# Attention with a state, then a two-layer MLP: weights cast by POOL from an fp32 staging ring, all loads on one queue

## The chip, the cores and the metric

The kernel runs on one core of one Trainium2 chip. The time is device microseconds of one execution; the figure for the kernel before is the median of three runs. A core has TensorE (PE in the profile), VectorE (DVE), ScalarE (ACT), GpSimd (POOL) and SyncE (SP). DMAs are issued by SP, by ACT and by POOL, and are carried by 16 DMA engines that they share.

## The reference

For each of 8 batches and 8 heads there are 512 tokens `x` and 32 state rows `state`, 64 wide. The tokens read the states, the states read the tokens, and all results (544 rows of 512 per batch, 4352 in all) go through a two-layer MLP with a leaky ReLU. Everything that comes in is fp32.

```python
scores = scale * x @ state^T            # per batch and head, 512 x 32
a      = softmax(scores);   xread = a @ state
scores2 = scale * state @ x^T           # 32 x 512
a2     = softmax(scores2);  sread = a2 @ x
rows   = concat([xread, sread])         # 4352 x 512
h      = rows @ moe_w_in                # 512 x 2048
out    = maximum(0.01 * h, h) @ moe_w_out   # 2048 x 512
```

## The kernel before, in words

The weights stay in SBUF as bf16 for the whole run: `w_in_bf` (128 partitions, 4 row blocks, 2048 columns) and `w_out_bf` (16 row blocks of 128 rows, 512 columns). The first product is folded: for each batch `a_m` multiplies the states by a 512-column chunk of w_in (line 389), which gives `M`, and `ff1` then multiplies `M` by the probabilities `aT` (line 410), so that xread itself is never formed. `piece` (line 438) does a quarter of the second product, four row blocks of w_out for one tile of 128 tokens. The 256 rows of sread go through `ff1_s` (line 421) at the end.

The instructions of every engine are in the order written in the code (a manual schedule); semaphores are put in by the framework. Batch 0 is done in a start-up of its own: four loads `xf` of 256 KB on SP, cast by VectorE (line 139), transposed on TensorE, scores, row maxima that are split into two bf16 parts `hi` and `lo` (lines 535 and 538), exponentials, probabilities. Between these come `a_m` for batches 0 and 1 as the four column chunks of w_in arrive, `ff1_0`, and then, for batch 1, two casts of `x1` by VectorE (line 687), transposes on TensorE (line 705, tile `pxt`), and the scores (line 253). From there on the loop over batches 2 to 7 runs 16 steps each: `ff1`, one piece of an earlier or of this batch, and at set steps the attention of the next batch. x of batch 2 is cast by ScalarE, that of later batches by POOL (`cast_all`, line 132), and its transpose is a DMA on SP. The states of batches 2 and 3 come by eight small loads on SP (`load_state(0)`, line 201), are scaled by VectorE (line 207) and transposed by a DMA (`st_t`, line 212).

At the start POOL issues the loads, in this order: four of w_in, each 512 rows by 512 columns; w_out row blocks 0 to 1; x of batch 1 in two halves (`x1`); w_out 2 to 3 and 4 to 7; first half of x of batch 2; w_out 8 to 11; second half of x of batch 2; w_out 12 to 13 and 14 to 15. The weight loads change fp32 to bf16 in the transfer, straight into `w_in_bf` and `w_out_bf`. x of batches 3, 4 and 5 is loaded on SP in one piece of 1 MB, that of 6 and 7 on POOL. Stores of the output are SP's.

Of the kernel before, what the change touches and what calls it, by code (L numbers as in the profile page):

```python
# [27 lines left out]
def kernel(  # L28
# [24 lines left out]
    VEC, SCA, POO = nc.vector.tensor_copy, nc.scalar.copy, nc.gpsimd.tensor_copy  # L53
# [5 lines left out]
    nc.scalar.dma_start(  # L59
        st0f[:], state[0:2].rearrange("b h n d -> (b h n) d").rearrange("(p r) d -> p r d", r=4)  # L60
    )
    xf = [consts.tile([P, 2, 2 * P], FP32, name="xf", tag=f"xf{q}") for q in range(NK)]
    xv = x[0].rearrange("h (p t) d -> p h (t d)", t=NT)
    for q in range(NK):
        nc.sync.dma_start(xf[q][:], xv[:, 2 * q:2 * q + 2])

    idle = consts.tile([P, S], BF16, name="idle")
    nc.vector.memset(idle[:], 0.0)
# [24 lines left out]
    w_in_bf = wpool.tile([P, NK, DFF], BF16, name="w_in_bf")  # L93
    w_out_bf = wpool.tile([P, 16, DM], BF16, name="w_out_bf")
    xs, xt, xl = {}, {}, {}

    def load_x(b, eng):
        xl[b] = xpool.tile([P, H, NT * D], FP32, name="xl", tag="xl", bufs=2)
        eng.dma_start(xl[b][:], x[b].rearrange("h (p t) d -> p h (t d)", t=NT))

    def load_x_half(b, u):
        if u == 0:
            xl[b] = xpool.tile([P, H, NT * D], FP32, name="xl", tag="xl", bufs=2)
        nc.gpsimd.dma_start(
            xl[b][:, NK * u:NK * (u + 1)],
            x[b, NK * u:NK * (u + 1)].rearrange("h (p t) d -> p h (t d)", t=NT),
        )

    def open_xb(b):
        if b == 2:
# [8 lines left out]
        h = 2 * (k % 2)  # L121
        return a.xb[k // 2][:, t, h:h + 2, :].rearrange("p h d -> p (h d)")

    def cast_x(b, h0, h1, copy):
        u = h0 // NK
        copy(
            xs[b][u][:, :, h0 - NK * u:h1 - NK * u].rearrange("p t h d -> p h t d"),
            xl[b][:, h0:h1].rearrange("p h (t d) -> p h t d", t=NT),
        )

    def cast_all(b):
        nc.gpsimd.tensor_copy(  # L132
            xt[b][:].rearrange("p t h d -> p h t d"),
            xl[b][:].rearrange("p h (t d) -> p h t d", t=NT),
        )

    def cast_x0(q, copy):
        v = q % 2
        copy(
            xs[0][q // 2][:, :, 2 * v:2 * v + 2].rearrange("p t h d -> p h t d"),  # L140
            xf[q][:].rearrange("p h (t d) -> p h t d", t=NT),
        )

    def load_w_in(c):
        nc.gpsimd.dma_start(  # L145
            w_in_bf[:, :, DM * c:DM * (c + 1)],
            moe_w_in[:, DM * c:DM * (c + 1)].rearrange("(k p) f -> p k f", p=P),
        )

    def load_w_out_rows(j0, j1):  # L150
        nc.gpsimd.dma_start(  # L151
            w_out_bf[:, j0:j1, :], moe_w_out[P * j0:P * j1, :].rearrange("(j p) f -> p j f", p=P)
        )

    def load_w_out(c):
        load_w_out_rows(4 * c, 4 * (c + 1))

    def spin(n, tag, w=S):
        p = psum.tile([P, S], FP32, name="pspin", tag=tag, bufs=2 if tag in ("ph", "py") else 1)
# [59 lines left out]
    def a_open(a, b):  # L219
        a.b = b  # L220
        a.xb = xs[b]
        if b == 2:
            t = att.tile([P, 2, NT, 2, P], BF16, name="xT", tag="xT")
            a.xTh = [t[:, u] for u in range(2)]
        else:
            t = att.tile([P, NT, NK, P], BF16, name="xT", tag="xT")
            a.xTh = [t[:, :, 2 * u:2 * u + 2] for u in range(2)]
        a.xT = t
# [7 lines left out]
    def a_xt_half(a, u):  # L236
        nc.sync.dma_start_transpose(
            a.xTh[u].rearrange("p t k q -> p (t k) q"),
            a.xb[u].rearrange("p t h d -> p (t h d)"),
        )  # L240
# [28 lines left out]
    def block_sub(flat, m1, n):  # L269
        m1b = att.tile([P, n, NS], FP32, name="mrowb", tag="mrowb", bufs=1)  # L270
        nc.vector.transpose(m1b[:], m1[:, :, None].to_broadcast([P, n, NS]))  # L271
        sh = att.tile([P, n * NS], FP32, name="sh", tag="sh")
        nc.vector.tensor_tensor(  # L273
            out=sh[:], in0=flat, in1=m1b[:].rearrange("p c j -> p (c j)"), op=ALU.subtract,
        )
        return sh
# [100 lines left out]
    def a_m(a, c, tag):  # L377
        if c == 0:
            a.M = mpool.tile([P, 2, DFF], BF16, name="M", tag="M")
        if tag in ("ph", "py", "phpy"):  # L380
            pm = [psum.tile([P, DM], FP32, name="pm", tag=t) for t in (tag[:2], tag[-2:])]
            at = [t[:] for t in pm]
        else:
            pm = psum.tile([P, 2, DM], FP32, name="pm", tag=tag, bufs=1)
            at = [pm[:, g, :] for g in range(2)]
        for k in range(NK):
            for g in range(2):
                v, r = (k // 2, 2 * (k % 2) + (g ^ (k // 2))) if a.b == 0 else (g, k)
                nc.tensor.matmul(  # L389
                    at[v][NS * r:NS * (r + 1)],  # L390
                    lhsT=st_of(a, g, k),
                    rhs=w_in_bf[D * g:D * (g + 1), k, DM * c:DM * (c + 1)],
                    start=True, stop=True,
                )
# [80 lines left out]
    a0, a1, a2 = att_of[:3]  # L475
# [91 lines left out]

    for c in range(4):
        load_w_in(c)
    load_w_out_rows(0, 2)  # L570
    x1 = [consts.tile([P, NK, 2 * P], FP32, name="x1", tag=f"x1{u}") for u in range(2)]
    for u in range(2):
        nc.gpsimd.dma_start(  # L573
            x1[u][:], x[1, NK * u:NK * (u + 1)].rearrange("h (p t) d -> p h (t d)", t=NT)
        )
    load_w_out_rows(2, 4)
    load_w_out(1)
    load_x_half(2, 0)
    load_w_out(2)
    load_x_half(2, 1)  # L580
    for v in range(2):
        load_w_out_rows(12 + 2 * v, 14 + 2 * v)
    a0.aT = att.tile([P, 2, S], BF16, name="aT", tag="aT")
    open_xb(1)
    a_open(a1, 1)
    for q in range(2):
        cast_x0(q, VEC)
# [24 lines left out]
    q = [recip0(0)]  # L612
# [62 lines left out]
    for j, tag in ((4, "ph"), (6, "big"), (8, "py"), (10, "big"), (12, "py"), (14, "ph")):  # L675
        t, bk = open_ff1_0(tag)
# [7 lines left out]
            m_halves(a0, 3, "ph")  # L684
            a_max2(a0)
    for u in range(2):
        VEC(  # L687
            a1.xb[u].rearrange("p t h d -> p h t d"),
            x1[u][:].rearrange("p h (t d) -> p h t d", t=NT),
        )  # L690
    nc.vector.memset(stf[0][:, 0, D - 1:D + 1], 0.0)
    load_state(0)

# [6 lines left out]
    for u in range(2):  # L700
        ps = psum.tile([P, NT, 2, P], BF16, name="pxt2", tag="ph")
        for t in range(NT):
            for v in range(2):
                h = NK * u + 2 * v
# [14 lines left out]
        piece(0, h0, i, 1)  # L719
    open_xb(2)  # L720
    a_open(a2, 2)
    cast_x(2, 0, 4, SCA)
    a_xt_half(a2, 0)
    m_evict(a1, 2, a_m(a1, 2, "ph"), SCA)
    a_exp(a1)
    for i in (2, 3):
        piece(0, h0, i, 1)
    m_evict(a1, 3, a_m(a1, 3, "ph"), SCA)
    cast_x(2, 4, 8, SCA)
    for g in range(2):  # L730
        a_exp2(a1, g)
    a_xt_half(a2, 1)
# [49 lines left out]
    for b in range(2, B):  # L782
        hT = hpool.tile([P, 16, S], BF16, name="hT", tag="hT")
# [58 lines left out]

    hs = hpool.tile([P, 16, B * NS], BF16, name="hs", tag="hs", bufs=1)
    b = B - 1
    order = [(0, 3), (1, 3), (2, 0), (2, 1), (2, 2), (2, 3)]
    for s in range(8):
# [41 lines left out]
```

## Time and profile before

| | us |
|---|---|
| three runs, median (lowest to highest) | 216.83 (216.08 to 217.03) |
| profiled execution: span of its instructions | 214.6 |
| median of the runs less that span (start and end around the instructions) | 2.2 |
| TensorE busy in it | 206.1 (96%) |
| ScalarE, VectorE, POOL busy in it | 139.1, 97.7, 25.4 |
| weight and x loads that POOL issues at the start: issue of the first, of the last | 2.83, 21.93 |

The profiled execution's own time is known by its span, 214.6 us; the runs stand 2.2 us above it. In a row of the timeline the first number is the start in us from the span's begin, the second the duration; "x4" says that four instructions are merged, and a bracket tells how long the engine had stood idle and what ended that. In the table by windows the columns are the stretch, its length, busy time of PE, weight loads, DVE, ACT and POOL with their instruction counts, the granted clock, the share of the 16 DMA engines that was busy, and GB/s moved. A row of a DMA on POOL or SP shows the issue; the landing is later. Bytes of a casting transfer are counted as they land, in bf16.

### The profile page before, as it was taken

Reading aid. Unit: us, or ns where it says so; the run is one execution under the profiler, and the core shown is the slowest. Engines: PE = TensorE matmul, PEld = TensorE weight load, DVE = VectorE, ACT = ScalarE, POOL = GpSimd, SP = SyncE. Lnnn points to the kernel's source line nnn. Section 1 sums busy time; section 2 is a strip of 40 time slices with the busy share of each in tenths; the row PEclk is TensorE's granted clock in tenths of the full one; section 3 lists DMA queues with packets and bytes.
Section 4 is the critical chain, followed back from the end, with each engine's and each line's share of the span. In section 5 each row is a group of like instructions: output and inputs, shape, how many; then the busy total and the mean of one; then the engine's idle time right before and its main releaser. Section 6 shows DMA issues by size and latency. Waiting matters only on the chain.

```text
span 214.6 us, 3685 instructions
## 1 busy us (share of the span) xinstructions
PE 206.1 (96%) x1479; PEld 96.5 (45%) x1504; DVE 97.7 (46%) x149; ACT 139.1 (65%) x263; POOL 25.4 (12%) x39
## 2 busy tenths in 40 slices
PE   7789999999999999999999999999999999999993
PEld 2533434344454444444444444444444455466542
DVE  2666687698748235741784095706580000000001
ACT  3578675898788476856696579647774756464420
POOL 8724100030032040521000000000000000000000
PEclk9999999999999999999999999999999999999999
DMA  6999999576992987394216321422124110111113
GB/s 205 207 206 295 257 253 113 126 270 124 241 217 79 200 243 244 89 276 89 87 52 138 59 99 52 100 47 101 48 68 79 74 74 2 49 52 49 49 49 101
DMA packets 38400, 27.70 MB, mean 129 GB/s; under 512 B 24560, under 2 KB 33136, under 8 KB 38384
## 3 DMA queue, kind: packets, MB, share of 16 engines
q1 hardware_dynamic: 32864, 18.95, 35.4%
q0 software_dynamic: 5376, 8.39, 17.4%
q8 instruction: 12, 0.20, 0.4%
q10 hardware_dynamic: 144, 0.13, 0.3%
q14 instruction: 4, 0.03, 0.1%
HBM read 17.30 MB, written 8.91 MB: 122 GB/s over the span
## 4 chain that ended last, share of the span: by engine, by line
PE 86%; DMA 7%; POOL 3%; ACT 1%; issue 1%; DVE 0%; POOLq 0%; ACTq 0%
PE py L438 50%; PE ph L410 22%; DMA x<-in_x_dram 7%; PE ph L421 3%; PE pm L389 3%; PE pyw L438 3%; PE psr L362 2%; PE pyh L462 2%; POOL w_in_bf L145 1%; PE sc L253 1%; ACT M L403 0%; ACT hT L415 0%; POOL x L573 0%; POOL w_out_bf L151 0%; DVE xb L687 0%
## 5 line engine op out<-in xcount | busy, mean ns | idle before, releaser
L438 PE MATMUL py<-w_out_bf,hT 128*128 128x512 bf16 x446 | 116.7, 380 | 1.0
L415 ACT ACTIVATE hT<-ph 128x512 bf16<-128x512 f32 x112 | 66.5, 602 | 41.7 <-PE ph L410 41.0
L438 PEld LDWEIGHTS <-hT 128*128 128x128 bf16 x496 | 46.7, 98 | 57.2 <-issue 5.3
L410 PE MATMUL ph<-aT,M 128*128 128x512 bf16 x221 | 64.9, 379 | 0.2
L410 PEld LDWEIGHTS <-M 128*128 128x128 bf16 x224 | 21.7, 98 | 27.1 <-issue 1.4
L447 ACT COPY ysb<-py 128x512 f32<-128x512 f32 x31 | 18.1, 585 | 10.7 <-PE py L438 10.7
L263 DVE TRANSPOSE_TENSOR_REDUCE mrow<-sc 128x32 f32<-128x1024 f32 x7 | 8.8, 1250 | 33.7 <-PE sc L253 33.7
L467 DVE COPY ysh<-pyh 128x384 f32<-128x384 f32 x1 | 0.6, 557 | 49.0 <-PE pyh L462 49.0
L132 POOL CAST xb<-xl 128x2048 bf16<-128x2048 f32 x5 | 9.4, 1890 | 58.9 <-DMA xl<-in_x_dram 48.2
L285 DVE TRANSPOSE_TENSOR_REDUCE r<-e 128x32 f32<-128x1024 bf16 x7 | 8.7, 1245 | 11.9 <-ACT e L280 11.9
L403 ACT CAST M<-pm 128x1024 bf16<-128x1024 f32 x13 | 13.2, 1013 | 1.2 <-PE pm L389 0.7
L319 ACT ACTIVATE e<-sc,mcol 128x512 bf16<-128x512 f32 x16 | 11.2, 706 | 0.0
L313 DVE TENSOR_REDUCE mcol<-sc 128x2 f32<-128x1024 f32 x8 | 9.7, 1214 | 0.0
L425 ACT ACTIVATE hs<-ph 128x256 bf16<-128x256 f32 x16 | 6.0, 384 | 4.6 <-PE ph L421 4.4
L294 DVE STREAM_TRANSPOSE qb<-qh 128x1024 bf16<-128x1024 bf16 x7 | 8.7, 1245 | 0.2
L271 DVE STREAM_TRANSPOSE mrowb<-mrow 128x1024 f32<-128x1024 f32 x7 | 8.7, 1245 | 0.2
L273 DVE TENSOR_TENSOR sh<-sc,mrowb 128x1024 f32<-128x1024 f32 x7 | 8.6, 1225 | 0.2
L401 DVE CAST M<-pm 128x512 bf16<-128x512 f32 x10 | 6.4, 686 | 4.9 <-PE pm L389 4.9
L403 DVE CAST M<-pm 128x1024 bf16<-128x1024 f32 x7 | 8.5, 1215 | 0.0
L421 PE MATMUL ph<-sr_t,w_in_bf 128*128 128x256 bf16 x64 | 8.3, 273 | 0.0
L438 PE MATMUL pyw<-w_out_bf,hT 128*128 128x512 bf16 x31 | 7.7, 380 | 0.1
L389 PE MATMUL pm<-w_in_bf,st_t 64*32 64x512 bf16 x192 | 7.6, 379 | 0.0
(97 smaller groups left out, 158.0 us busy)
## 6 DMA issues: line engine op xcount, KB each, us to landing
out_dram<-ysb SPq DMA_DIRECT2D x31, 256.0 KB, 2.4
xl<-in_x_dram SPq DMA_DIRECT2D x3, 1024.0 KB, 6.6
w_in_bf<-in_moe_w_in_dram POOLq DMA_DIRECT2D x4, 512.0 KB, 10.4
xl<-in_x_dram POOLq DMA_DIRECT2D x2, 1024.0 KB, 6.7
xf<-in_x_dram SPq DMA_DIRECT2D x4, 256.0 KB, 3.8
w_out_bf<-in_moe_w_out_dram POOLq DMA_DIRECT2D x4, 256.0 KB, 13.9
x<-in_x_dram POOLq DMA_DIRECT2D x2, 512.0 KB, 15.3
w_out_bf<-in_moe_w_out_dram POOLq DMA_DIRECT2D x2, 512.0 KB, 15.4
```

Of the source, the lines that this page charges most:

```text
L132: nc.gpsimd.tensor_copy(xt[b][:].rearrange("p t h d -> p h t d"), xl[b][:].rearrange("p h (t d) -> p h t d", t=NT),)
L263: nc.vector.tensor_reduce(out=m1[:], in_=flat.rearrange("p (c j) -> p c j", j=NS), axis=AX.X, op=ALU.max, apply_transpose=True,)
L271: nc.vector.transpose(m1b[:], m1[:, :, None].to_broadcast([P, n, NS]))
L313: nc.vector.tensor_reduce(out=a.m2[:], in_=a.sc[:], axis=AX.X, op=ALU.max, negate=True)
L319: nc.scalar.activation(out=a.e2[:, g], in_=a.sc[:, g, :], func=AF.Exp, bias=a.m2[:, g:g + 1], accum_out=a.r2[:, g:g + 1],)
L389: nc.tensor.matmul(at[v][NS * r:NS * (r + 1)], lhsT=st_of(a, g, k), rhs=w_in_bf[D * g:D * (g + 1), k, DM * c:DM * (c + 1)], start=True, st ...
L403: copy(a.M[:, :, cols], pm[:])
L410: nc.tensor.matmul(ph[:], lhsT=a.M[:, g, P * j:P * (j + 1)], rhs=a.aT[:, g, :], start=(g == 0), stop=(g == 1),)
L415: nc.scalar.activation(out=hT[:, j, :], in_=ph[:], func=AF.Prelu, scale=1 / SCALE, alpha=0.01)
L421: nc.tensor.matmul(ph[:, :n], lhsT=w_in_bf[:, k, P * j:P * (j + 1)], rhs=sr_t[:, k, :], start=(k == 0), stop=(k == NK - 1),)
L438: nc.tensor.matmul(y.py, lhsT=hT[:, j, P * i:P * (i + 1)], rhs=w_out_bf[:, j, :], start=(j == 0), stop=(j == 15),)
L447: copy(ysb[:], ys[b, i].py)
```

## The change

All start-up loads go to SP and arrive as fp32. A pool `ring` of eleven buffers, each 4 KB a partition (512 KB), takes the place of `xf`, `x1` and `xl`. A weight load is a half of the former w_in chunk (two row blocks by 512 columns) or two row blocks of w_out; POOL then casts it from the ring into `w_in_bf` or `w_out_bf`. The order of the tensors is the old one: w_in in eight halves, w_out 0 to 1, x of batch 1 in two halves, w_out 2 to 7, half of x of batch 2, w_out 8 to 11, the other half, w_out 12 to 15; then SP's list goes on with the states of batches 2 and 3. x of every batch is now loaded and cast in two halves, on the queues and engines as before but for those that left POOL's start-up list. A buffer of the ring is loaded again when its cast is done: `x1`'s first half waits for VectorE's casts of `xf`, the loads from w_out 2 on for POOL's casts of w_in. The tile `sh` has one buffer instead of two, and `hs` shares the two buffers of `hT`.

```diff
+    ring = ctx.enter_context(tc.tile_pool(name="ring", bufs=11))
+    HALF = NK * 2 * P
+    def stage():
+        return ring.tile([P, HALF], FP32, name="ring", tag="ring")
+    def x_half(b, u, eng):
+        t = stage()
+        eng.dma_start(t[:].rearrange("p (h c) -> p h c", h=NK),
+            x[b, NK * u:NK * (u + 1)].rearrange("h (p t) d -> p h (t d)", t=NT))
+        return t
+    xf = [stage() for _ in range(2)]
...
     def load_x(b, eng):
-        xl[b] = xpool.tile([P, H, NT * D], FP32, name="xl", tag="xl", bufs=2)
-        eng.dma_start(xl[b][:], x[b].rearrange("h (p t) d -> p h (t d)", t=NT))
+        for u in range(2):
+            load_x_half(b, u, eng)
...
+    def weights(dst, src):
+        t = stage()
+        v = t[:].rearrange("p (j f) -> p j f", j=2)
+        nc.sync.dma_start(v, src)
+        nc.gpsimd.tensor_copy(dst, v)
     def load_w_in(c):
-        nc.gpsimd.dma_start(
-            w_in_bf[:, :, DM * c:DM * (c + 1)],
-            moe_w_in[:, DM * c:DM * (c + 1)].rearrange("(k p) f -> p k f", p=P),
-        )
+        cols = slice(DM * c, DM * (c + 1))
+        v = moe_w_in[:, cols].rearrange("(k p) f -> p k f", p=P)
+        for k in range(0, NK, 2):
+            weights(w_in_bf[:, k:k + 2, cols], v[:, k:k + 2])
...
-        sh = att.tile([P, n * NS], FP32, name="sh", tag="sh")
+        sh = att.tile([P, n * NS], FP32, name="sh", tag="sh", bufs=1)
...
     for c in range(4):
         load_w_in(c)
-    load_w_out_rows(0, 2)
-    x1 = [...]
-    load_w_out_rows(2, 4)
-    load_w_out(1)
-    load_x_half(2, 0)
-    load_w_out(2)
-    load_x_half(2, 1)
-    for v in range(2):
-        load_w_out_rows(12 + 2 * v, 14 + 2 * v)
+    load_w_out(0, 2)
+    load_x(1, nc.sync)
+    load_w_out(2, 8)
+    load_x_half(2, 0, nc.sync)
+    load_w_out(8, 12)
+    load_x_half(2, 1, nc.sync)
+    load_w_out(12, 16)
...
-    hs = hpool.tile([P, 16, B * NS], BF16, name="hs", tag="hs", bufs=1)
+    hs = hpool.tile([P, 16, B * NS], BF16, name="hs", tag="hT")
```

More of the change, by code (lines that the diff above doesn't have):

```diff
@@ L61 @@
     )
-    xf = [consts.tile([P, 2, 2 * P], FP32, name="xf", tag=f"xf{q}") for q in range(NK)]
+    ring = ctx.enter_context(tc.tile_pool(name="ring", bufs=11))
[4 more added lines that the diff above has]
+        t = stage()
+        eng.dma_start(
+            t[:].rearrange("p (h c) -> p h c", h=NK),
+            x[b, NK * u:NK * (u + 1)].rearrange("h (p t) d -> p h (t d)", t=NT),
+        )
+        return t
+    xf = [stage() for _ in range(2)]
     xv = x[0].rearrange("h (p t) d -> p h (t d)", t=NT)
     for q in range(NK):
-        nc.sync.dma_start(xf[q][:], xv[:, 2 * q:2 * q + 2])
+        v = q % 2
+        nc.sync.dma_start(
+            xf[q // 2][:, S * v:S * (v + 1)].rearrange("p (h c) -> p h c", h=2),
+            xv[:, 2 * q:2 * q + 2],
+        )
     idle = consts.tile([P, S], BF16, name="idle")
@@ L97, in load_x, with load_x_half @@
     def load_x(b, eng):
-        xl[b] = xpool.tile([P, H, NT * D], FP32, name="xl", tag="xl", bufs=2)
-        eng.dma_start(xl[b][:], x[b].rearrange("h (p t) d -> p h (t d)", t=NT))
-    def load_x_half(b, u):
-        if u == 0:
-            xl[b] = xpool.tile([P, H, NT * D], FP32, name="xl", tag="xl", bufs=2)
-        nc.gpsimd.dma_start(
-            xl[b][:, NK * u:NK * (u + 1)],
-            x[b, NK * u:NK * (u + 1)].rearrange("h (p t) d -> p h (t d)", t=NT),
-        )
+        for u in range(2):
+            load_x_half(b, u, eng)
+    def load_x_half(b, u, eng):
+        xl[b, u] = x_half(b, u, eng)
     def open_xb(b):
@@ L122, in pair_of, with cast_x @@
         return a.xb[k // 2][:, t, h:h + 2, :].rearrange("p h d -> p (h d)")
-    def cast_x(b, h0, h1, copy):
-        u = h0 // NK
+    def cast_x(b, u, copy):
         copy(
-            xs[b][u][:, :, h0 - NK * u:h1 - NK * u].rearrange("p t h d -> p h t d"),
-            xl[b][:, h0:h1].rearrange("p h (t d) -> p h t d", t=NT),
+            xs[b][u].rearrange("p t h d -> p h t d"),
+            xl[b, u][:].rearrange("p (h t d) -> p h t d", h=NK, t=NT),
         )
     def cast_all(b):
[L132 to L135, printed above, removed]
+        for u in range(2):
+            cast_x(b, u, nc.gpsimd.tensor_copy)
     def cast_x0(q, copy):
@@ L140, in cast_x0, with load_w_out @@
             xs[0][q // 2][:, :, 2 * v:2 * v + 2].rearrange("p t h d -> p h t d"),
-            xf[q][:].rearrange("p h (t d) -> p h t d", t=NT),
+            xf[q // 2][:, S * v:S * (v + 1)].rearrange("p (h t d) -> p h t d", h=2, t=NT),
         )
-    def load_w_in(c):
-        nc.gpsimd.dma_start(
-            w_in_bf[:, :, DM * c:DM * (c + 1)],
-            moe_w_in[:, DM * c:DM * (c + 1)].rearrange("(k p) f -> p k f", p=P),
[L148 to L156, printed above, removed]
+    def weights(dst, src):
[3 more added lines that the diff above has]
+        nc.gpsimd.tensor_copy(dst, v)
+    def load_w_in(c):
+        cols = slice(DM * c, DM * (c + 1))
+        v = moe_w_in[:, cols].rearrange("(k p) f -> p k f", p=P)
+        for k in range(0, NK, 2):
+            weights(w_in_bf[:, k:k + 2, cols], v[:, k:k + 2])
+    def load_w_out(j0, j1):
+        v = moe_w_out.rearrange("(j p) f -> p j f", p=P)
+        for j in range(j0, j1, 2):
+            weights(w_out_bf[:, j:j + 2, :], v[:, j:j + 2])
     def spin(n, tag, w=S):
@@ L569 @@
         load_w_in(c)
-    load_w_out_rows(0, 2)
[L571 to L575, printed above, removed]
-    load_w_out_rows(2, 4)
-    load_w_out(1)
-    load_x_half(2, 0)
-    load_w_out(2)
-    load_x_half(2, 1)
-    for v in range(2):
-        load_w_out_rows(12 + 2 * v, 14 + 2 * v)
+    load_w_out(0, 2)
[5 more added lines that the diff above has]
+    load_w_out(12, 16)
     a0.aT = att.tile([P, 2, S], BF16, name="aT", tag="aT")
@@ L686 @@
     for u in range(2):
[L687 to L690, printed above, removed]
+        cast_x(1, u, VEC)
     nc.vector.memset(stf[0][:, 0, D - 1:D + 1], 0.0)
@@ L721 @@
     a_open(a2, 2)
-    cast_x(2, 0, 4, SCA)
+    cast_x(2, 0, SCA)
     a_xt_half(a2, 0)
@@ L728 @@
     m_evict(a1, 3, a_m(a1, 3, "ph"), SCA)
-    cast_x(2, 4, 8, SCA)
+    cast_x(2, 1, SCA)
     for g in range(2):
```

## The prediction

> **What bounds the kernel now.** I read the page first, then the chain in order of time for the first 45 us, then the timeline of that stretch, then busy time by window.
>
> ```profile
> span 214.6 us, 3685 instructions
> ...
> PE 206.1 (96%) x1479; PEld 96.5 (45%) x1504; DVE 97.7 (46%) x149; ACT 139.1 (65%) x263; POOL 25.4 (12%) x39
> ...
> PE 86%; DMA 7%; POOL 3%; ACT 1%; issue 1%; DVE 0%; POOLq 0%; ACTq 0%
> ```
>
> TensorE is busy for 206.1 of 214.6 us. The whole program cannot gain more than the 8.5 us between them, and the chain gives DMA only 7%. The next view says where that 7% lies.
>
> ```profile
> 7.40 15.65 DMA x<-in_x_dram
> 23.05 0.02 issue
> 23.07 0.69 DVE xb L687
> ...
> 23.82 0.62 PE pxt L705 x8
> ```
>
> It is one piece: the second half of batch 1's x (line 573) lands at 23.05, stands in its queue behind all of w_in, and VectorE's cast and TensorE's transposes follow it. After that the chain is TensorE almost alone. So only the first 41 us can be touched by how inputs arrive; they are a race between TensorE and the loads. TensorE's side of the race, the starts that need a new input:
>
> ```profile
> 10.72 0.41 PE L389 MATMUL pm<-w_in_bf,stbd 64*32 64x512 bf16 x8
> ...
> 12.76 0.41 PE L389 MATMUL pm<-w_in_bf,stbd 64*32 64x512 bf16 x8 [0.24 <-DMA w_in_bf<-in_moe_w_in_dram]
> ...
> 16.39 0.41 PE L389 MATMUL pm<-w_in_bf,stbd 64*32 64x512 bf16 x8 [0.52 <-DMA w_in_bf<-in_moe_w_in_dram]
> ...
> 18.93 0.41 PE L389 MATMUL pm<-w_in_bf,stbd 64*32 64x512 bf16 x8
> ...
> 22.89 0.61 PE L705 MATMUL pxt<-ident,xb 128*128 128x128 bf16 x8
> ...
> 23.82 0.62 PE L705 MATMUL pxt<-ident,xb 128*128 128x128 bf16 x8 [0.33 <-DVE stf L691]
> ...
> 25.14 0.59 PE L438 MATMUL pyw<-w_out_bf,hT 128*128 128x512 bf16 x2
> ```
> ```profile
> 26.67 2.75 PE L438 MATMUL py<-w_out_bf,hT 128*128 128x512 bf16 x11
> ...
> 31.86 1.90 PE L438 MATMUL py<-w_out_bf,hT 128*128 128x512 bf16 x8
> ...
> 33.60 3.62 PE L438 MATMUL pyw<-w_out_bf,hT 128*128 128x512 bf16 x15
> ...
> 40.60 0.41 PE L253 MATMUL sc<-xT,st_t 64*32 64x512 bf16 x8
> ```
>
> The four w_in column chunks are needed at 10.72, 12.76, 16.39 and 18.93; the second and third came late by 0.24 and 0.52. By the order of the pieces in the code, w_out's rows 2 to 3 are needed at 25.14, rows 4 to 7 near 27.6 (three matmuls into the row at 26.67), rows 8 to 11 at 31.86, rows 14 and 15 near 36.2 (the last four of the row at 33.60). At 40.60 batch 2's scores need its transposed x and states.
>
> **The stream of loads.** What leaves: 14 issues by POOL (four for w_in, six for w_out, four for x), the weights cast on the way. What comes: 20 loads of 512 KB in fp32 on SP (16 of weights, four of x), in the same order of tensors, behind the four xf loads. How fast is SP's queue in fp32?
>
> ```profile
> 3.00:5.00 2.00, 1.92 (x16) 0.67 (x15) 0.76 (x2) 0.23 (x1) 2.00 (x3) 1.00 1.08 373
> 8.00:12.00 4.00, 3.08 (x112) 1.96 (x112) 2.30 (x10) 1.95 (x5) 1.70 (x3) 1.00 1.24 206
> 44.75:46.50 1.75, 1.75 (x9) 0.74 (x8) 1.75 (x3) 1.59 (x3) 1.39 (x1) 1.00 1.06 402
> 74.50:77.00 2.50, 2.50 (x13) 1.15 (x12) 0.00 (x0) 1.04 (x3) 0.00 (x0) 1.00 1.10 351
> ```
>
> The last column is GB/s. From 8 to 12 us the casting transfers land 206 GB/s of bf16, which is 412 of fp32 read: the number to hold. SP's queue moves 373 (xf) and 351 (xl) when x comes in rows of 1 KB, and 402 where the output is stored in rows of 2 KB. The trace has no fp32 load in rows of 2 KB, which is what the weights are. The row it is nearest to by length is the store, so I take 402 for the weights, 1.30 us a half, and 360 for x, 1.46 us. The low end is 351 for all, 1.49 us. There is a lower one, not taken:
>
> ```profile
> xl<-in_x_dram SPq DMA_DIRECT2D x3, 1024.0 KB, 6.6
> xf<-in_x_dram SPq DMA_DIRECT2D x4, 256.0 KB, 3.8
> ```
>
> 768 KB more take 2.8 us more, 281 GB/s; but those loads start on a queue that had stood idle or full of transposes, and the xf stream that the new loads join does not.
>
> ```profile
> 4.28 0.47 DVE L139 CAST xb<-xf 128x512 bf16<-128x512 f32 x1 [0.33 <-DMA xf<-in_x_dram]
> 6.46 0.46 DVE L139 CAST xb<-xf 128x512 bf16<-128x512 f32 x1 [0.24 <-DMA xf<-in_x_dram]
> ...
> L132 POOL CAST xb<-xl 128x2048 bf16<-128x2048 f32 x5 | 9.4, 1890 | 58.9 <-DMA xl<-in_x_dram 48.2
> ```
>
> xf lands one by one from 4.28 to 6.46, so the stream's clock stands at 6.44 when it ends, and each half adds its term. POOL's cast of 2048 elements takes 1.89 us; 1024 take 0.95, and I allow 1.1 with the two hand-overs. It is under 1.30, so POOL keeps up and adds 1.1 once behind each landing, not a sum of sixteen. Ready times: w_in chunks 6.44 + 2 x 1.30 + 1.1 = 10.14, then 12.74, 15.34, 17.94. Batch 1's x (nine weight halves, then two of x, no POOL cast) lands at 21.06, against 23.05. Then w_out rows 2-3 are ready at 23.5, 4-7 at 26.1, 8-11 at 30.1, 14-15 at 34.2. Against the needs, nothing is late, the 0.52 at 16.39 goes, and so does batch 1's x. What is late next is TensorE itself: the first transposes go at 22.89 - 0.52 = 22.37, the second at once behind them when VectorE has cast the second half (22.85), and that is 23.82 - 22.85 = 0.97 us won. That would be all of the gain: from there TensorE has no gap.
>
> **What POOL's casts do to VectorE.** Between 7.8 and 19 us POOL is now casting 0.95 of every 1.30 us, where it issued DMAs. Has VectorE paid for POOL before?
>
> ```profile
> 6.62 1.59 POOL L573 DMA_DIRECT2D x<-in_x_dram  x2
> ...
> 7.74 0.48 DVE L535 CAST hi<-m 128x16 bf16<-128x16 f32 x1
> ...
> 9.59 0.17 DVE L535 CAST hi<-m 128x16 bf16<-128x16 f32 x1
> ...
> 9.80 0.18 DVE L538 TENSOR_TENSOR lo<-m,hi 128x16 bf16<-128x16 f32 x1
> ```
> ```profile
> 65.83 1.59 POOL L207 TENSOR_SCALAR stb<-stf 128x512 bf16<-128x512 f32 x1 [2.96 <-DMA stf<-in_state_dram]
> ...
> 65.98 0.57 DVE L327 TENSOR_SCALAR r<-r 128x2 f32<-128x2 f32 x1
> ```
> ```profile
> L327 DVE TENSOR_SCALAR r<-r x8: 160/163/573, 38.5 to 157.4; 128x2 f32<-128x2 f32 x8
> ```
>
> Twice: `hi` took 0.48 beside a busy POOL and 0.17 beside an idle one, and the one slow `r` of eight (573 against 163 ns) began 0.15 us into a POOL instruction. So a small VectorE operation beside POOL costs 0.3 to 0.4 more, and at most the rest of the POOL cast, 0.95. The two splits (`hi`, `lo`, at 7.74 and 9.59) lie on TensorE's way to the first w_in product at 10.72. The first half lands at 7.74, so POOL's first two casts run about 7.85-8.8 and 9.15-10.1. I take one block of 0.6 that stays: the first `lo` waits to 8.85, the maxima behind it slip, and the second split then falls into the gap after the second cast. Bounds 0 and 1.5 (both casts in full, less the gap).
>
> The Trainium skill (SBUF — State Buffer, "Who interferes with whom") says that a cast or a two-input operation of VectorE and any GpSimd operation take one port pair as an exclusive lock for the whole instruction, the first to start winning. By that the block would be the rest of the cast, 0.6 here; the two slow rows above fit it, though 0.57 is less than the 1.59 of the POOL instruction beside it.
>
> With the 0.6, the first product goes at 11.3, the second at 13.1 (12.76 less its wait of 0.24, plus 0.6), the third at 16.23, 0.16 before its old time, and the second transposes follow the first at 22.73 + 0.61 = 23.35 instead of 23.82. Net gain 0.47 us.
>
> **Behind the stream on SP.** The state loads of batches 2 and 3 and the transposes of batch 2 had SP to themselves; now they stand behind the weights.
>
> ```profile
> SPq L237 <- DMA stf<-in_state_dram: 1.3, 1, 1.3
> ...
> L237 SPq DMA_TRANSPOSE xT<-xb x2: 1232/1280/1329, 29.3 to 34.0; - x2
> ...
> L212 SPq DMA_TRANSPOSE st_t<-stb x2: 1190/1788/2385, 36.0 to 67.4; - x2
> DMA to landing us min/median/max: 2.4/3.0/3.5
> ```
>
> SP does wait for an earlier DMA's landing before it reuses its semaphore (the 1.3 us). In the changed kernel's list of SP's instructions the eighth state load waits in this way for the last weight half, landing at 33.1. Two half transposes of 1.28 follow, to 36.1, then st_t with 1.2 to 2.4 of issue, landed by 39.0 to 39.6. Needed at 40.60 - 0.47: hidden with 0.5 us to spare. If the stream is late by more, TensorE is late by the weights as well, so this does not add. VectorE's state cast waits with it, with output copies queued behind; they are due after 37. The load of batch 3's x starts about when it did.
>
> **At no cost.** `sh` with one buffer: its reader, the exponential, is done a batch earlier. `hs` in the hT ring takes the buffer of batch 6, whose last piece is ten steps before. Later casts in two halves of 0.95 instead of one of 1.89, and double issues on POOL for batches 6 and 7, run a batch ahead. If these covers went, each would cost under 1 us.
>
> **The sum.** 214.6 - 0.47 = 214.1 of span. The median of the runs, 216.83, is 2.2 us above the profiled span; that part is not touched. Forecast 216.4 us. 0.5% (1.08 us) is about what a measurement of this kernel can tell from no change; the runs before lie 0.95 us apart.
>
> **The rivals.** *No block.* If POOL's casts miss the splits, the gain is the 0.97: 215.9. For it: other POOL casts leave VectorE's long operations at their usual length; against: the two slow rows.
>
> *The slow stream (slower).* If 2 KB fp32 rows move like x, 351 GB/s, each half takes 1.49: the last w_out rows are ready at 6.44 + 20 x 1.49 + 1.1 = 37.3 instead of the needed 36.2, so 1.1 to 1.2 us are lost and TensorE waits in steps from 25.14 on: 218.0. It decides from (36.2 - 1.1 - 6.44) / 20 = 1.43 us a half. For it: every fp32 load in the trace is at 351 to 373, and one queue without a second beside it has nothing to fill a pause; against: those are 1 KB rows. The far end, 281 GB/s, would give about 8 us. The skill (DMA: Bandwidth & Descriptors, "Where 436 GB/s comes from") puts reads from HBM at about 358 GB/s; by it the loss would be some 0.7 us, 217.5, but the trace reads 412.
>
> *POOL becomes the bound (slower).* If a cast takes over 1.30 us beside busy neighbours, POOL paces the weights. The row at 65.83 shows one POOL operation on 512 elements at 1.59. At 1.9 a half the fourth chunk of w_in is ready at 7.85 + 8 x 1.9 = 23.05, 4.1 us after 18.93: 221. Against it: five casts of 1.89 for 2048 elements, within 0.01.
>
> *The change does nothing*, because the race is decided elsewhere: 216.8.
>
> **How the numbers follow.** Forecast 0.36, no block 0.20, slow stream 0.29, POOL 0.10, nothing 0.05. Faster by over 0.5% (under 215.75): 0.02 of the forecast and 0.12 of the no-block case, which lies near that line, 0.14. Slower: 0.24 of the slow stream, 0.10 of POOL, 0.02 of the rest, 0.36. Same 0.50. The range 215.6 to 219.0 leaves out 0.06 below and 0.14 above (POOL and the stream's far end). The likeliest case alone: 215.9 to 216.9.
>
> **What would show it.** Right: 512 KB loads landing every 1.3 to 1.5 us from 7.7 on, L389 without a DMA or POOL wait at the third chunk, the second pxt directly behind the first, `lo` long, no wait at 31.86 or 40.60. Wrong: POOL waited for by L389 or L438, L253 waiting for st_t, POOL casts over 1.3 us, or a gap of TensorE after 41 us that was not there.

## The result, and the profile after

The changed kernel takes 219.53 us, median of four runs (218.99 to 220.42), against 216.71 (216.08 to 217.03) for the kernel before on the same chip: ratio 1.013, 95% interval 1.0087 to 1.0173. Forecast were 216.4 us and a range of 215.6 to 219.0, so it is slower than forecast and outside the range. A second set of runs, on another chip, gave 219.48 against 215.92, ratio 1.0151 (1.0093 to 1.0209). The loss is 2.8 us in one set and 3.6 in the other; the intervals overlap. Some executions, two of the six of the changed kernel in that second set among them, ran at a lower granted clock and took longer; medians and ratios here and below are of the others.

The page of the changed kernel, first three lines of totals, then the chain by engine and by line:

```profile
span 217.1 us, 3728 instructions
...
PE 206.9 (95%) x1479; PEld 96.8 (45%) x1504; DVE 97.4 (45%) x149; ACT 139.3 (64%) x263; POOL 33.8 (16%) x48
...
PE 76%; DMA 17%; SPq 2%; ACT 1%; issue 1%; POOL 1%; DVE 0%; ACTq 0%
```

TensorE does nearly the same work (206.9 against 206.1 us); the span grew by 2.5, so TensorE idles 1.7 us more. POOL's busy time grew by 8.4 us, and its share of the chain is 1%: POOL is not the bound. DMA has 17% of the chain where it had 7%. The chain in order of time says which DMAs (start, duration, what):

```profile
4.81 8.97 DMA ring<-in_moe_w_in_dram
13.78 11.28 DMA ring<-in_moe_w_out_dram
...
25.67 10.78 DMA ring<-in_moe_w_out_dram
...
36.51 1.23 POOL w_out_bf L156
...
37.78 1.04 PE pyw L449 x4
...
38.85 0.90 DVE ysb L458 x2
39.75 3.21 DMA st_t<-stb
...
43.01 0.41 PE sc L264 x8
```

Until 36.46 the chain is the stream of weight loads; then one cast by POOL, one piece on TensorE, and `st_t`, which batch 2's scores (now line 264) wait for. TensorE's rows at the places where the prediction put its needs:

```profile
14.17 0.40 PE L400 MATMUL pm<-w_in_bf,stbd 64*32 64x512 bf16 x4 [0.62 <-POOL w_in_bf L156]
17.79 0.40 PE L400 MATMUL pm<-w_in_bf,stbd 64*32 64x512 bf16 x4 [0.20 <-POOL w_in_bf L156]
...
24.44 1.10 PE L707 MATMUL pxt<-ident,xb 128*128 128x128 bf16 x16
...
37.78 1.02 PE L449 MATMUL pyw<-w_out_bf,hT 128*128 128x512 bf16 x4 [0.34 <-POOL w_out_bf L156]
...
43.01 0.41 PE L264 MATMUL sc<-xT,st_t 64*32 64x512 bf16 x8 [0.74 <-DMA st_t<-stb]
```

Three waits on POOL and one on `st_t` stand where the prediction had none. Batch 2's scores go at 43.01 instead of 40.60, 2.41 late, and that is the 2.5 of the span. The waits at 37.78 and 43.01 both count: the end of that piece is 38.80 against 33.60 + 3.62 = 37.22 before, 1.58 late, and 0.74 is added at `st_t`.

SP's list shows what held `st_t`; the last row is VectorE's scaling of the states:

```profile
36.48 0.31 SPq L212 DMA_DIRECT2D stf<-in_state_dram  x1
36.90 2.76 SPq L248 DMA_TRANSPOSE xT<-xb  x2
39.75 2.07 SPq L223 DMA_TRANSPOSE st_t<-stb  x1
```
```profile
38.19 0.29 DVE L218 TENSOR_SCALAR stb<-stf 128x256 bf16<-128x256 f32 x1 [1.35 <-DMA stf<-in_state_dram]
```

The eighth state load goes out at 36.48, just behind the last weight landing. The two transposes of batch 2's x stand behind it, and `st_t` behind them. The scaled states were ready at 38.48, 1.27 before `st_t` was issued, so it was SP's order that held it and not the states' data. By the landing times of the trace the second transpose of x landed at 42.70, only 0.26 before `st_t`: an earlier `st_t` alone would have won little more than that (an estimate; no run moved it alone).

POOL's rows are a clock of the landings, because each cast starts 0.05 us behind its landing where POOL is free:

```profile
10.37 1.04 POOL L156 CAST w_in_bf<-ring 128x1024 bf16<-128x1024 f32 x1 [0.24 <-DMA ring<-in_moe_w_in_dram]
11.73 1.03 POOL L156 CAST w_in_bf<-ring 128x1024 bf16<-128x1024 f32 x1 [0.32 <-DMA ring<-in_moe_w_in_dram]
13.09 1.03 POOL L156 CAST w_in_bf<-ring 128x1024 bf16<-128x1024 f32 x1 [0.32 <-DMA ring<-in_moe_w_in_dram]
15.34 1.04 POOL L156 CAST w_in_bf<-ring 128x1024 bf16<-128x1024 f32 x1 [1.22 <-DMA ring<-in_moe_w_in_dram]
16.70 1.03 POOL L156 CAST w_in_bf<-ring 128x1024 bf16<-128x1024 f32 x1 [0.33 <-DMA ring<-in_moe_w_in_dram]
...
36.51 1.22 POOL L156 CAST w_out_bf<-ring 128x1024 bf16<-128x1024 f32 x1 [0.22 <-DMA ring<-in_moe_w_out_dram]
```

The casts follow each other by 1.36 us, the pace of the loads, with one step of 2.25 between 13.09 and 15.34: a pause of 0.9 in the stream. Each cast takes 1.03 to 1.04 (the last one 1.22), so a half is ready about 1.1 behind its landing. The last weight half lands at 36.46; the forecast was 33.08.

The same clock for the kernel before, POOL's issues that waited for a casting transfer to land:

```profile
10.46 0.78 POOL L151 DMA_DIRECT2D w_out_bf<-in_moe_w_out_dram  x1 [1.54 <-DMA w_in_bf<-in_moe_w_in_dram]
13.01 0.75 POOL L106 DMA_DIRECT2D xl<-in_x_dram  x1 [1.77 <-DMA w_in_bf<-in_moe_w_in_dram]
16.62 0.74 POOL L151 DMA_DIRECT2D w_out_bf<-in_moe_w_out_dram  x1 [2.86 <-DMA w_in_bf<-in_moe_w_in_dram]
19.17 0.75 POOL L106 DMA_DIRECT2D xl<-in_x_dram  x1 [1.80 <-DMA w_in_bf<-in_moe_w_in_dram]
```

Chunks of 1 MB landed 2.55, 3.61 and 2.55 us apart: a pause of 1.06 before the third chunk was already there, and it made the wait of 0.52 at 16.39. By the landing times of the trace the first chunk came at 10.18, 3.74 after the last `xf` (6.44), where two halves of 1.27 make 2.54: a gap of 1.2 at the start was there too. The changed stream has both again (0.95 and 0.9). Against these landings it is late by little, 0.3 us at the second and third chunk of w_in (13.03 and 16.65 against 12.72 and 16.34) and 1.0 at the last rows of w_out (36.46 against 35.46). The cast adds its 1.1 to that.

### The profile page after: what moved, and what is told of

It is laid out like the page before. It is cut to its first block, busy times and chain, and to the rows that moved or that the text cites. A ratio compares the mean times of both kernels' runs of the same rounds, so it can differ in the third digit from the quotient of the medians.

```text
span 217.1 us, 3728 instructions
## 1 busy us (share of the span) xinstructions
PE 206.9 (95%) x1479; PEld 96.8 (45%) x1504; DVE 97.4 (45%) x149; ACT 139.3 (64%) x263; POOL 33.8 (16%) x48
## 4 chain that ended last, share of the span: by engine, by line
PE 76%; DMA 17%; SPq 2%; ACT 1%; issue 1%; POOL 1%; DVE 0%; ACTq 0%
PE py L449 46%; PE ph L421 21%; DMA ring<-in_moe_w_out_dram 10%; DMA ring<-in_moe_w_in_dram 4%; PE ph L432 3%; PE pm L400 3%; PE psr L373 2%; DMA st_t<-stb 1%; PE sc L264 1%; SPq L155 1%; SPq L80 1%; POOL w_out_bf L156 1%; DMA out_dram<-ysb 1%; SPq L462 1%; PE pyw L449 0%
## 5 line engine op out<-in xcount | busy, mean ns | idle before, releaser
L426 ACT ACTIVATE hT<-ph 128x512 bf16<-128x512 f32 x112 | 66.5, 602 | 42.1 <-PE ph L421 41.5
L136 POOL CAST xb<-ring 128x1024 bf16<-128x1024 f32 x10 | 10.4, 1038 | 40.4 <-DMA ring<-in_x_dram 37.4
L156 POOL CAST w_out_bf<-ring 128x1024 bf16<-128x1024 f32 x8 | 8.5, 1059 | 8.8 <-DMA ring<-in_moe_w_out_dram 8.8
L156 POOL CAST w_in_bf<-ring 128x1024 bf16<-128x1024 f32 x8 | 8.3, 1035 | 9.3 <-DMA ring<-in_moe_w_in_dram 9.3
```

The source lines that it names most:

```text
L136: copy(xs[b][u].rearrange("p t h d -> p h t d"), xl[b, u][:].rearrange("p (h t d) -> p h t d", h=NK, t=NT),)
L156: nc.gpsimd.tensor_copy(dst, v)
L426: nc.scalar.activation(out=hT[:, j, :], in_=ph[:], func=AF.Prelu, scale=1 / SCALE, alpha=0.01)
```

## The experiments

The theory I tested: three late events hang on the stream and each is a bound of its own. The start-up chunks wait for landing plus cast (about 1.1 us), w_out's last rows wait in the same way (0.5 more), and `st_t` stands in SP's list behind the state loads and so behind the last weight landing (0.8 more). Rivals: VectorE held by POOL's casts; the other edits; the pace and start of SP's queue. Times are medians; "before" is that of the same set of runs. The sets were run on different chips, so a variant is compared with the changed kernel by the ratio of each to it.

**Casting the weights in the transfer again.** The ring (for x), the half casts of x, `sh` and `hs` stay as changed; the loads go back to POOL's queue, and w_in to whole column chunks.

```diff
...
-        nc.sync.dma_start(v, src)
-        nc.gpsimd.tensor_copy(dst, v)
+        nc.gpsimd.dma_start(dst, src)
...
-        for k in range(0, NK, 2):
-            weights(w_in_bf[:, k:k + 2, cols], v[:, k:k + 2])
+        weights(w_in_bf[:, :, cols], v)
...
```

> The core of the change undone alone: the weights go by POOL's queue and are cast in the transfer, x of batches 1 and 2 goes by POOL's queue into the ring in the old order; ring, half casts of x, one sh buffer and hs in the ring of hT stay. Theory of three waits: 214.4 to 214.8 of span, no difference from the kernel before, so the other edits cost nothing. Rival, the halves or the shared buffers cost: over 215.2.

Measured: 215.88 against 215.80, ratio 1.0015 (0.9984 to 1.0047); span 213.6. TensorE's rows:

```profile
21.90 1.23 PE L703 MATMUL pxt<-ident,xb 128*128 128x128 bf16 x16
...
39.29 0.41 PE L260 MATMUL sc<-xT,st_t 64*32 64x512 bf16 x8
```

No wait on a load is left. So the whole loss is that of the weights' new path, and the ring, the halves of x, `sh` and `hs` cost nothing that can be measured.

**The changed kernel again**, as the base of the comparisons that follow.

> The changed kernel as it is, beside the ones below on one chip, so that they can be compared with it. Expected: 1.011 to 1.018 of the kernel before, the scores of batch 2 on TensorE near 43.0 us.

Measured: 219.48 against 215.92, span 217.7, with waits of 0.63 and 0.54 on POOL at the second and third chunk, 0.33 at the last piece, and 0.72 for `st_t` before the scores at 43.31.

**The state loads between the last weight loads.**

```diff
-    load_w_out(2, 8)
+    for n, j in enumerate((2, 4, 6)):
+        load_w_out(j, j + 2)
+        load_state_one(0, n)
...
```

(and so on to row 14; `load_state(0)` behind them goes).

> One part moved: the eight state loads of batches 2 and 3 stand one by one between the last weight loads on SP's queue instead of behind all of them, so that none of them waits for the last weight half to land. Theory of three waits (the loss of 2.5 us of span is 1.1 from POOL's hand-over at the w_in chunks, 0.5 at the last w_out half, and 0.8 at st_t, all in line): st_t lands before TensorE wants it, the wait of 0.74 us at the scores of batch 2 goes, span 216.2 to 216.4. Rival, the stream alone is slow and everything behind it moves with it: span stays at 217.1, the 0.8 us turns up elsewhere.

Measured: 218.67 against 215.80, ratio 1.0137 (1.01 to 1.0173), span 216.6, 0.2 above the range given.

```profile
38.14 1.02 PE L454 MATMUL pyw<-w_out_bf,hT 128*128 128x512 bf16 x4 [0.31 <-POOL w_out_bf L156]
...
42.55 0.41 PE L269 MATMUL sc<-xT,st_t 64*32 64x512 bf16 x8
```

The scores wait for nothing any more, but they start only 0.5 to 0.8 earlier, because TensorE comes to them late from the last rows of w_out (these landed at 37.00, with small loads now ahead of them in the queue and a first half that was 0.35 later). These are two bounds of nearly one height.

**Loads and casts in quarters of 256 KB.**

```diff
-        nc.sync.dma_start(v, src)
-        nc.gpsimd.tensor_copy(dst, v)
+        for j in range(2):
+            nc.sync.dma_start(v[:, j:j + 1], src[:, j:j + 1])
+            nc.gpsimd.tensor_copy(dst[:, j:j + 1], v[:, j:j + 1])
```

> The hand-over halved: every weight half is loaded in two pieces of 256 KB and cast by POOL piece by piece (32 loads and 32 casts of about 0.55 us instead of 16 of 1.04). Theory of three waits: the last piece of each chunk is handed over 0.5 us sooner, the waits at the second and third chunk shrink, and st_t, which hangs on the last landing and not on TensorE, keeps the end where it was: span 217.0 to 217.2 with a longer wait at st_t. Rival, hand-over is all that was lost: 216.5. Rival, the queue is bound by its issues: later landings, over 217.6.

Measured: 219.74, ratio 1.0195 (1.0154 to 1.0236), span 217.6, above the 217.0 to 217.2 of the theory.

```profile
13.61 0.39 PE L401 MATMUL pm<-w_in_bf,stbd 64*32 64x512 bf16 x2 [0.29 <-POOL w_in_bf L157]
...
43.35 0.41 PE L265 MATMUL sc<-xT,st_t 64*32 64x512 bf16 x8 [1.63 <-DMA st_t<-stb]
```

The hand-over is half as long and the second chunk goes 0.5 earlier, but all of it turns into a longer wait for `st_t`: 1.63 instead of 0.72, and the scores where they were. It is the mirror image of the run before.

**Both.**

> The two experiments before this one put together: state loads between the last weight loads, and pieces of 256 KB. Each alone left the scores of batch 2 near 43 us, one because the last w_out half was handed over late (38.1), the other because st_t landed late (43.3). Theory of two bounds of nearly one height, both hung on the last landing at 36.5: together they bring the scores to 41.5-42.0 and the span to 0.8-1.3 us under the changed kernel's. Rival, the stream's end alone sets the time: under 0.4 us.

Measured: 218.91 against 215.92, ratio 1.0132 (1.0081 to 1.0183), span 216.4, which is 1.3 under the changed kernel's 217.7; the medians carry only 0.6 of that, and the intervals of the two ratios overlap, so the forecast gain of 0.8 to 1.3 is not shown. The scores go at 42.65, later than the 41.5 to 42.0 expected: a wait of 0.64 for w_out's rows came back at 37.29, and the last of them landed at 37.63, 1.0 later than in the changed kernel of that set.

**Each cast reads the half before its own** (the weights are shifted by a half, so the output is another). POOL has the same work, and a chunk is ready one landing sooner. Alone, and with the state loads between:

```diff
...
+        landed.append(v)
-        nc.gpsimd.tensor_copy(dst, v)
+        nc.gpsimd.tensor_copy(dst, landed[max(len(landed) - 2, 0)])
```

> The changed kernel, but each of POOL's casts reads the half that landed before its own (so the weights are shifted by one half and the output is another); POOL has the same casts, SP the same loads. So a chunk of weights is ready one landing, 1.1 to 2.2 us, earlier, and the hand-over to POOL no longer counts. Theory (two bounds that hang on the same last landing: the hand-over of w_out's last rows at about 42.2, the states' transpose at about 43.0): TensorE's waits for POOL at the w_in chunks and before pyw go, the first transposes of batch 1 come 1.0 to 1.4 us earlier, but batch 2's scores still wait for st_t and start at 42.5 to 43.3; the span is 0 to 0.5 us below the changed kernel's 217.1 to 217.7. Rival (the hand-over of the weights sets the end by itself): span 1.2 to 1.6 us lower, 216.0 or less.

> The same shift by one half, and the eight state loads issued between the last weight loads, so that both bounds are moved. Theory: batch 2's scores start with the end of w_out's pieces or with st_t's landing at 41.3 to 42.2; the span is 215.5 to 216.2, 1.5 to 2.0 us below the changed kernel. What is left above the kernel before (213.6 to 214.6) is the late landing of the stream itself. Rival (the loss lies in neither, for example in POOL's casts beside VectorE): span 217 or more.

Measured: alone 219.40 against 215.83 (span 217.5; ratio 1.0116, 0.9985 to 1.0247, too wide to say more); with the state loads 218.08, ratio 1.0123 (1.008 to 1.0166), span 215.7. Rows of the first, then of the second:

```profile
12.02 0.24 PE L531 MATMUL scn<-ident,lo 128*32 128x128 bf16 x4 [0.74 <-DVE lo L552]
...
43.37 0.41 PE L267 MATMUL sc<-xT,st_t 64*32 64x512 bf16 x8 [0.98 <-DMA st_t<-stb]
```
```profile
10.47 0.94 DVE L557 TENSOR_TENSOR lo<-m,hi 128x16 bf16<-128x16 f32 x1
```
```profile
23.36 1.24 PE L721 MATMUL pxt<-ident,xb 128*128 128x128 bf16 x16
...
28.54 1.46 PE L457 MATMUL py<-w_out_bf,hT 128*128 128x512 bf16 x6 [0.26 <-POOL w_out_bf L159]
...
41.64 0.41 PE L272 MATMUL sc<-xT,st_t 64*32 64x512 bf16 x8
```

Alone, TensorE waits nowhere for weights and the end is held by `st_t`, as expected. The transposes of batch 1 did not come earlier (25.07): that execution's last `xf` was 0.6 late, and VectorE's `lo` was held as well. With both moved, one wait of 0.26 for w_out's rows is left, the scores go unwaited at 41.64, and the span is 2.0 under the changed kernel's 217.7, inside the range given. Of that the medians carry 1.4, on another chip; by the two ratios (1.0123 and 1.0151) the gain is 0.6, and their intervals overlap.

**VectorE's part.** `hi` given to ScalarE:

```diff
-        VEC(hi[:], m[:])
+        SCA(hi[:], m[:])
```

> One operation moved: the cast hi of the row maxima is done by ScalarE, so that it cannot be held up by POOL's cast (0.80 us in the changed kernel, 0.17 without POOL beside it). Rival of the port: TensorE's first w_in product comes 0.5 to 0.6 us earlier and the span falls by as much, to 216.5. Theory of three waits: the product comes earlier, but the second chunk is then waited for longer (0.62 becomes about 1.2 us, POOL hands it over at 14.1 whatever VectorE does); span 217.0 to 217.1.

Measured: 220.0, ratio 1.0215 (1.0164 to 1.0267), span 217.9: no gain, and 0.8 above the span expected. `lo` came later behind ScalarE's `hi` and was held itself (0.71 us), so the first product went at 11.74, later than the 11.12 of the changed kernel. The second chunk had landed 0.44 earlier in this execution and went unwaited at 13.47, and 1.69 was lost at `st_t`. The run moves VectorE's block and does not remove it; what the block costs by itself is not shown by it.

In the shifted kernel the hold does show, since nothing else is late there. There POOL's second cast has no landing to wait for and stands right behind the first, so that `lo` is held too. The last run lets the first two casts read their own halves, so that the shift begins with the third:

> The kernel with the shift by one half and the state loads between the weight loads, but the first two casts read the half that they belong to (the shift begins with the third, so the output is still another than the reference's). POOL's second cast then waits for its landing again instead of standing right behind the first, and VectorE's lo slips in between: lo 0.18 instead of 0.94, the first w_in product at 11.0 to 11.4 instead of 12.16, batch 1's transposes at 22.2 to 22.7 instead of 23.36. Theory (what is left above the kernel before is the late landing of the stream's last part): the time won is lost again in waits for w_out's rows or for st_t, batch 2's scores start at 41.1 to 41.7 as in the run with both moved (41.64), span 215.2 to 215.8. Rival (what is left is POOL's hold on VectorE at the start): scores at 40.3 to 40.8, span 214.3 to 214.9.

Measured: 218.08 against 215.75, ratio 1.0105 (1.0025 to 1.0184), span 215.8, scores at 41.65. The number is the theory's, but not for its reason. In this execution the pause fell before the last `xf` (7.68 instead of 6.67), `lo` was held again (0.91), the first w_in product went at 12.61, and from there TensorE waited for no load at all. So it does not tell lock and stream apart; it shows that with both waits gone a late start (12.61 instead of 10.72 for the first product) goes with an end that is 1 us late.

**The gap at the start of the stream, and its pace.** An early read of 256 bytes from each of w_in's first 256 rows, on ScalarE's queue:

```diff
+    touch = consts.tile([P, 2, D], FP32, name="touch")
+    nc.scalar.dma_start(touch[:],
+        moe_w_in[0:2 * P, 0:D].rearrange("(k p) f -> p k f", p=P))
```

> One small load more: ACT's queue reads 256 bytes of each of w_in's first 256 rows at the start, ahead of the stream. In the changed kernel the first weight half lands 2.3 us behind the last xf load, though later ones are 1.35 apart, and single packets there take up to 0.8 us. Theory that a first access to those rows is slow: the first half lands 1.4-1.6 behind xf, everything after it 0.7 sooner, span 0.5-0.7 under the changed kernel's. Rival, the gap belongs to the change from one load to the next or to that moment: no difference, within 0.3.

Measured: 220.94, ratio 1.0217 (1.017 to 1.0263), span 218.7, so 1.0 above the changed kernel in place of no difference; the first half still landed 2.37 after the last `xf` (9.31 after 6.94). Touching a part of each of these rows early does not shorten the gap.

The fp32 halves issued on POOL's queue, six ahead of the casts:

```diff
...
-        nc.sync.dma_start(v, src)
-        nc.gpsimd.tensor_copy(dst, v)
+        if len(casts) >= ahead:
+            cast_next()
+        nc.gpsimd.dma_start(v, src)
+        casts.append((dst, v))
...
```

> The same fp32 halves into the same ring with the same POOL casts, but issued on POOL's queue instead of SP's, six loads ahead of the casts; POOL's issues and casts then share one engine, so the end comes later than in the changed kernel (222 to 228) and only the landings of the first seven halves are of use. If the pace of 1.355 us a half and the start gap of 2.3 us belong to SP's queue: halves land every 1.25 to 1.31 us and the first within 1.4 us of the last xf. If they belong to fp32 being written (512 KB where the casting transfer writes 256): 1.34 to 1.40 us a half here too.

Measured, one run: 223.02, span 221.1. By the landing times of the trace the third to the eighth half come at 12.20, 13.50, 15.48, 16.84, 18.19 and 19.55, and the first 2.40 after the last `xf`. Pace, gap and pause (13.50 to 15.48) are nearly the same on the other queue, so none of them belongs to SP. The pace of 1.355 goes with transfers that land in fp32; the casting ones, also on POOL's queue, take 1.27 a half. Gap and pause do not: the casting transfers of the kernel before have both. What makes them stays open.

**POOL's casts left out**, and the weights filled by eight POOL memsets at the start:

```diff
+    for c in range(4):
+        nc.gpsimd.memset(w_in_bf[:, :, DM * c:DM * (c + 1)], 0.01)
+    for j in range(0, 16, 4):
+        nc.gpsimd.memset(w_out_bf[:, j:j + 4, :], 0.01)
...
-        nc.gpsimd.tensor_copy(dst, v)
```

> POOL's sixteen casts of weights are left out (the bf16 weights are filled with a constant at the start instead, so the result is not the product with the weights); the loads into the ring run as in the changed kernel. TensorE then waits for no weights at all. Theory that the wait at st_t stands in for the others, as it hangs on SP's queue and the last landing alone: TensorE comes to the scores of batch 2 over 1 us sooner and waits there, span within 0.4 us of the changed kernel's. Rival, the casts and their hand-over are the loss: span falls by 1.5 to 2.5 us.

Measured: 228.46, ratio 1.0568 (1.052 to 1.0617), span 225.9. As a test of the casts it failed, because the memsets cost more than the casts they replaced. VectorE's row and POOL's two:

```profile
3.64 13.46 DVE L494 TENSOR_SCALAR stb<-st0f 128x256 bf16<-128x256 f32 x1 [2.50 <-DMA st0f<-in_state_dram]
```
```profile
2.95 7.04 POOL L115 MEMSET w_in_bf<- 128x2048 bf16 x4
9.92 7.04 POOL L117 MEMSET w_out_bf<- 128x2048 bf16 x4
```

An operation that takes 0.29 on a like tile elsewhere stood for 13.46 us, until POOL's last memset ended.

**What the times alone say.** Of these variants only the one that casts in the transfer (1.0015) is set apart from the changed kernel (1.013 and 1.0151) on the fast side; the intervals of the others with a ratio, memsets aside, overlap those of the changed kernel. That the weights' new path makes the loss is shown by the times. How it divides among hand-over, landings and SP's list is read from the rows of one execution each.

## Why the prediction was wrong

**What bounds the kernel now: right.** It is a race of TensorE and the loads over the first 41 us. All of the loss lies in it.

**The stream's clock: the step that failed.** "xf lands one by one ..., so the stream's clock stands at 6.44 when it ends, and each half adds its term." The last weight half was to land at 6.44 + 16 x 1.30 + 4 x 1.46 = 33.08 and landed at 36.46. Of the 3.4 us, 0.2 are a later `xf` (6.67), 1.1 the pace (1.355 a weight half and 1.50 an x half), 0.95 the gap behind `xf`, 0.9 the pause, 0.2 the last loads. The pace was a term mis-sized by 4%. Gap and pause were left out, though the kernel before has both. The same model applied to its own first chunk gives 6.44 + 2 x 1.27 = 8.98 for a chunk that landed at 10.18, and the quoted wait of 0.52 at 16.39 is the pause. I had held an ideal stream against needs measured beside a real one. Against the landings before, the right sum is short: chunks and rows land 0.3 to 1.0 later and are ready another 1.1 later, 1.4 at the second chunk (14.12 against 12.72) and 2.3 at the last rows (37.73 against 35.46).

**POOL's cast: right.** Forecast 0.95 and a hand-over of 1.1 once behind each landing; measured 1.03 to 1.04 and 1.1; POOL never paces the weights. But "nothing is late" followed from the clock: the second chunk, forecast ready at 12.74, was ready at 14.12, and TensorE had already waited 0.24 for it before the change. A need that waits for its load has no slack for a hand-over.

**The gain of 0.97 up to batch 1's x: half of it came, under a larger loss.** The second transposes do follow the first at once, as forecast (one row of 16 at 24.44), but 1.55 later than 22.89. At the piece behind them TensorE is only 1.09 late (25.37 against 24.28), so 0.46 was won there. The 0.52 at the third chunk was not: TensorE is 1.4 late ahead of it and behind it.

**VectorE's block: right in size, in part by luck, and without effect.** Two rows of the second split:

```profile
9.36 0.80 DVE L546 CAST hi<-m 128x16 bf16<-128x16 f32 x1
10.20 0.18 DVE L549 TENSOR_TENSOR lo<-m,hi 128x16 bf16<-128x16 f32 x1
```

`hi` takes 0.80 instead of 0.17, so 0.63 for the forecast 0.6; the first product goes at 11.12 (forecast 11.3). Then TensorE waits 0.62 for the second chunk all the same; no run took the block away alone, so that it costs nothing is read from these rows. The forecast had POOL's first cast at 7.85, against the first `lo`; it came at 9.10, against the second `hi`, so that the size agrees is luck. The Trainium skill (SBUF — State Buffer, "Who interferes with whom") has it as a lock for the whole instruction, and for an operation with two inputs, like `lo`, only where POOL's reads SBUF, as these casts do. The rows agree: `hi` ends at 10.16, just as POOL's cast from 9.10 does (10.14). Of the two slow rows in the prediction, `r` does not bear it out: it ended 0.87 before the POOL operation beside it did. In the shifted kernel, with nothing else late, `hi` and `lo` together take 0.97 + 0.94.

**"This does not add": wrong.** From the last weight landing to `st_t`'s the forecast had 5.9 to 6.5 us and the run 6.50, so that chain was named and sized rightly. But it was taken to be covered whenever the stream is late, since TensorE is late then too. TensorE came 1.58 later than before, which is 2.05 later than forecast (the gain of 0.47 was not there); `st_t` landed 3.36 later than the forecast's 39.6. The difference, 1.3, less the spare 0.5 is 0.8: the wait of 0.74. The two run beside each other from one landing: the longer one counts, and removing one only uncovers the other, as the runs with state loads between and with quarters show.

**The other edits at no cost: right** (ratio 1.0015 with them alone).

**The rivals.** The slow stream was the nearest. Its 1.49 us a half is the average that came, (36.46 - 6.67) / 20, but that is luck: it came not by rows moving slowly but by 1.355 a half, plus gap and pause. It forecast the last rows ready at 37.3 (37.73) and a loss of 1.1 to 1.2 there (1.58), and it had no `st_t`. No block, POOL as the bound and no change are out.

**Slips in the sums.** The transposes are spaced by 0.48 in one sum (22.37 to 22.85) and by 0.61 in the other (22.73 to 23.35); the run has 1.10 for both. 281 GB/s costs 8.7 us by the sum that gives 1.1 for 351, not 8. The 2.2 us from span to run was 1.9 in each of the four runs of the changed kernel. None of these moves the forecast by more than 0.3.

## What to carry to other kernels

Cost a changed stream of loads by the difference to the landings in the trace of before, piece by piece, never by a start and a pace alone: first run the model over the old stream and see whether it gives the landings that are there. A consumer that already waits for its load pays every microsecond of a hand-over put behind it. When two chains leave the same late event, price both to their ends; each cure alone gains only the difference between them.

## What was not expected of the hardware

Eight POOL memsets that stand back to back kept VectorE out for all of them: 13.46 us for an operation of 0.3. Casts that stand back to back did not. In the shifted kernel with the state loads between, five follow each other without a pause:

```profile
9.38 5.01 POOL L159 CAST w_in_bf<-ring 128x1024 bf16<-128x1024 f32 x5 [6.49 <-DMA ring<-in_moe_w_in_dram]
```
```profile
9.47 0.97 DVE L554 CAST hi<-m 128x16 bf16<-128x16 f32 x1
```

`hi` ended at 10.44 and `lo` at 11.41, each held for about one cast of 1.03 and no longer. Where each cast waits for a landing, VectorE is held once (`hi` for 0.80 in the changed kernel). What sets the memsets apart was not tested.

Also, the stream of loads pauses for about 1 us: mostly at the third chunk of w_in (before, changed), but in the shifted kernel with the state loads between only at w_out's rows 2 to 3 (landed 2.78 behind the load before them), and in the last of the shifted runs already at `xf`. In the run with memsets, in which TensorE stood still until 17.16, w_in landed evenly at 1.36 a half. This was seen in the landings, and its cause was not tested.
